# Second batch's transposes one step later, ScalarE counting the experts' tokens, and some sums made by accumulating transfers

## The chip, the cores and the metric

One Trainium2 chip, of which one core is used. The time is the device time of one execution in microseconds (us). The kernel before has a median of 761.44 us over three runs (760.91 to 762.48).

## What is computed

Linear attention with an exponential feature map (4 batches, 8 heads, 576 tokens, head size 64), then a token-mixing sum and a feed-forward block, then a mixture of 8 experts in which every token's expert comes from a running choice. Cut to what matters here:

```python
x = attention(q, k, v, w_phi)                  # [4, 576, 512]
u = x + (x.T @ U @ V).T                        # token mixing, rank 32
x = u + relu(u @ w_ch1) @ w_ch2                # feed-forward, 2048 hidden
logits = x @ w_gate                            # 8 experts
e[s] = argmax(logits[s]) if local_gate[s] < 0.5 or s == 0 else e[s - 1]
out[s] = p[e] * (relu(x[s] @ w1[e]) @ w2[e])
```

## The kernel before

**Precision.** A matrix that goes to TensorE is split in two words: the high one is a copy rounded to the matmul's type, the low one is the value minus the high word. A product is three matmuls (high by high, high by low, low by high), recorded at L1169 to L1171 for the first products of a unit and L1495 to L1497 for the second ones. The high word is a copy on ScalarE (ACT), the low word a subtraction on VectorE (DVE) or GpSimd (POOL). For the experts' second weights (`w_end`, L389) there is already another way: ACT writes minus the high word into the low word's place (L387), and a transfer that POOL issues adds the value to it.

**Items.** The feed-forward block is 4 units of hidden columns times 3 tiles of 768 tokens: items 0 to 11. The experts are 4 batches times 2 units: items 12 to 19. An item is a row of steps. A step is one block product (12 matmuls) of the first layer or a group of 12 matmuls of the second. A seven-product scheme for 2 by 2 blocks replaces eight block products by seven in most items, at the price of sums and differences on DVE. In the last feed-forward unit (items 9, 10 and 11) the second layer uses it too: `seven_steps` and then `z_steps`, 14 steps of which each is a product of 384 columns. Item 12, the first of the experts, is plain: 16 steps with 288 columns.

**The end of a z item.** After the last product DVE adds PSUM and `u2` into the tile `u3` (L1457). What is then still missing in `y`, the block's output, is `u2` on one piece and `u3` on two pieces of 2 by 384 columns. `rest` adds them on DVE, 128x768 each (`from_sbuf`, L1410), and hands copies of `y` to the queue of SyncE (SP) (`sent`, L1415). In items 9 and 10 `rest` is run early in the next item, in item 11 at its end. `ys`, the copy in DRAM, is read only by a loop at the end that runs for batches with more than one expert.

**Routing.** `route(b)` finds batch b's experts in eleven parts: logits on TensorE (L1552), transposes (L1559), small DVE and ACT operations (L1576 to L1595), transposes back (L1606) with copies on ACT (L1610), a scan along the tokens on DVE (L1613), the count of each expert's tokens on DVE (L1617), a product (L1620), transfers (L1624 to L1628), and the choice of the expert (L1633). `PLANS[b]` gives for each part the step at which it is put into the programs of the engines, counted in sixteens from the batch's first item: items 10, 11, 12, 13 for batches 0 to 3. The second batch's part with L1606 stands at 21, that is item 12, step 5; the third batch's logits stand at 2, that is item 12, step 2, and read the tokens 1152 to 1727 of `y`.

**Order of the work.** The kernel is scheduled by hand. All engines' programs are written out in one pass. A planner in Python keeps a clock for each engine (`free`), for each buffer (`touched`) and for the DMA engines (`transfer`), and lets side work (weights, `x` blocks) into an engine's program at a step (`side`, `gate`, `either`) when its planned end is at most a slack behind TensorE's planned clock. `PLAN_COST` tells it what each part of the routing costs DVE, ACT and TensorE. Every engine then works through its program in order and waits at semaphores. `x_end` makes the high and low words of an `x` block; for the first expert batch (`("m", 0)`) there are four blocks of 128x576, made from `y`.

Of the kernel before, what the change touches and what calls it, by code (L numbers as in the profile page):

```python
# [8 lines left out]
F32R = mybir.dt.float32r  # L9
U32 = mybir.dt.uint32  # L10
I32 = mybir.dt.int32
ACTF = mybir.ActivationFunctionType
ALU = mybir.AluOpType
# [30 lines left out]
def model(ctx, tc, kq, vx, wphi, ident, up, vp, wff, wg, wmoe1, wmoe2, rconst, outT):  # L44
# [13 lines left out]
    def f32(ap):  # L58
        return ap.bitcast(F32)
# [14 lines left out]
    def paused(eng, **kw):  # L74

        eng.tensor_tensor(**kw)  # L76
        if eng is nc.gpsimd and pauses[0] and free["POOL"] >= landed[0]:
            nc.gpsimd.drain()
# [107 lines left out]
    def cost(eng, n):  # L186
        return {"DVE": 0.085 + n / 960, "ACT": 0.17 + n / 1330, "POOL": 0.05 + n / 340}[eng]
# [12 lines left out]
    def gate(eng, dur, *keys):  # L200

        if not late:
            yield "step"
        while late and not force[0]:
            at = max([free[eng], port[0] if eng == "DVE" else 0.0] + [touched.get(id(k), 0.0) for k in keys])
            if at + (0.0 if eng == "POOL" else dur) <= free["PE"] + SLACK[eng][at_step[0]]:
                break
            yield "wait"
        emitted[0] += 1
        force[0] = False  # L210
        if late:
            if eng == "DVE":
                free[eng] = max(free[eng], port[0])
            at = book(eng, dur, *keys)
            if eng == "DVE":
                port[0] = at

    def either(eng, n, *keys):

        if not late:  # L220
            yield "step"
            emitted[0] += 1
            return eng
        while True:
            best = None
            for e, name, bias in ((nc.gpsimd, "POOL", 0.0), (nc.vector, "DVE", BIAS)):
                dur = cost(name, n)
                at = max([free[name], port[0]] + [touched.get(id(k), 0.0) for k in keys])
                ok = (name == "DVE" or not lean[0]) and at + (0.0 if name == "POOL" else dur) <= free["PE"] + SLACK[name][at_step[0]]
                if (ok or force[0] and (name == "DVE" or not lean[0])) and (best is None or at + dur + bias < best[0]):  # L230
                    best = (at + dur + bias, e, name, dur)
            if best is not None:
                break
            yield "wait"
        emitted[0] += 1
        force[0] = False
        free[best[2]] = max(free[best[2]], port[0])
        port[0] = book(best[2], best[3], *keys)
        return best[1]

    def transfer(kb, at=None):

        wire[0] = max(free["PE"] if at is None else at, wire[0]) + kb / 400
        return wire[0] + 2.5
# [394 lines left out]
    def spot(key, s):  # L639
# [2 lines left out]
        w = CH if key[0] == "m" else TW  # L642
        return slice(2 * k, 2 * k + 2), slice((2 * key[1] + t) * w, (2 * key[1] + t + 1) * w)

    def x_end(key, s, r, keep, own=None, then=None):

        x = xo.setdefault(key, {})[s] = yield from take(xfree)
        wanted[1] -= then is not None and key[0] == "f"
        n_ = CH if key[0] == "m" else TW
        keys = (x,) if own is None else (x, own)  # L650
        yield from gate("ACT", cost("ACT", 2 * n_), *keys)
        nc.scalar.copy(out=x[:, 0, :, :n_], in_=r)
        for k in (slice(0, 2),) if late else (slice(0, 1), slice(1, 2)):
            use = yield from either(nc.gpsimd, n_ * (k.stop - k.start), *keys)
            paused(use, out=x[:, 1, k, :n_], in0=r[:, k], in1=f32(x[:, 0, k, :n_]), op=ALU.subtract)
        if keep:
            def send():
                nc.sync.dma_start(out=f32(xd[key[1]][XD.index(s)]), in_=f32(x))
                if late:
                    transfer(768)  # L660
            later(x, send)
        xdone.add((key, s))
        if then is not None:
            then()

    def as_x(r):
        return r.rearrange("p (k t) -> p k t", k=2)
# [533 lines left out]
    def seven_steps(i):  # L1201
# [140 lines left out]

        late["rest"] = rest

    def z_item(i):
        return items[i][0].kind == "ffn" and items[i][0].g in ZU

# [29 lines left out]
    def z_steps(i):  # L1377

        u, b = items[i]
        zr, zx = zd["zr"], zd["zx"]  # L1380
        p1, u3 = late["u2"], late["u3"]
        at, done = {}, {}

        def ys(r, t):
            t0 = (2 * b + t) * TW
            return y[:, 2 * r:2 * r + 2, t0:t0 + TW]

        def product(w, x, name, first):
            wt, xt_ = need_w(u, "z" + w), zx[x]
            for j in range(2):  # L1390
                if first:
                    ps, m = bank()
                    done[name, j] = (ps[:, :TW], m)
                    free["PE"] = max(free["PE"], ps_at[m])
                ps, m = done[name, j]
                if not first:
                    free["PE"] = max(free["PE"], ps_at[m])
                at[name, j] = three(ps, wt, xt_, j, first, True, True)
            if last[u] == i:
                wfree.append(u.w.pop("z" + w))  # L1400
            (hfree if any(zx[x] is h for h in hall) else xfree).append(zx.pop(x))

        def to_y(name, r, t):
            for j in range(2):
                ps, m = done[name, j]
                dst = ys(r, t)[:, j]
                ps_at[m] = dve(TW, at[name, j], out=dst, in0=ps, in1=dst, op=ALU.add)

        def from_sbuf(src, r, t, op=ALU.add):
            dve(2 * TW, 0.0, src, out=ys(r, t), in0=ys(r, t), in1=as_x(src), op=op)  # L1410

        def sent(r):
            for d in (2 * r, 2 * r + 1):
                ts_ = slice(2 * b * TW, (2 * b + 2) * TW)
                waiting.append((free["DVE"] + SYNC, lambda d=d: nc.sync.dma_start(out=late["ys"][:, d, ts_], in_=y[:, d, ts_])))  # L1415

        product("A11", "B11", "a", True)
        yield
        for j in range(2):
            ps, m = done["a", j]  # L1420
            ps_at[m] = act(lambda: nc.scalar.copy(out=p1[j], in_=ps), TW, at["a", j])
        touched[id(late["u2w"])] = ps_at[m]
        z_sub("T2", "B22", "T1")
        rows.append(zr.pop("T1"))
        z_high("T2")
        product("S1", "T1", "e", True)
        yield
        to_y("e", 1, 0)
        zd["less"]("T4", "e", "T2")
        z_high("T4")  # L1430
        z_low("T2")
        rows.append(zr.pop("T2"))
        product("A12", "B21", "a", False)
        yield
        zd["less"]("T3", "d", "B22")
        rows.append(zr.pop("B22"))
        z_high("T3")
        z_low("T4")
        rows.append(zr.pop("T4"))
        to_y("a", 0, 1)  # L1440
        product("S4", "B22", "e", False)
        yield
        to_y("e", 0, 0)
        z_low("T3")
        rows.append(zr.pop("T3"))
        product("S2", "T2", "b", True)
        yield
        to_y("b", 0, 0)
        product("A22", "T4", "d", True)
        yield  # L1450
        to_y("d", 1, 1)
        product("S3", "T3", "b", False)
        yield
        assert not zr and not zx
        for j in range(2):
            ps, m = done["b", j]
            ps_at[m] = dve(TW, at["b", j], late["u3w"], out=u3[j], in0=ps, in1=p1[j], op=ALU.add)  # L1457

        def rest(part):
            if part == 0:  # L1460
                from_sbuf(late["u2w"], 0, 0)
                sent(0)
            else:
                for t in range(2):
                    from_sbuf(late["u3w"], 1, t)
                sent(1)

        zd["rest"] = rest
        if not (i + 1 < n and z_item(i + 1)):
            for part in range(2):  # L1470
                z_rest(part)
# [71 lines left out]
    def route(b):  # L1543
# [70 lines left out]
        yield  # L1614

        cnt = small("cnt", [8, 1])
        nc.vector.tensor_reduce(out=cnt, in_=ta, axis=AX, op=ALU.add)  # L1617
        yield

        nc.vector.tensor_tensor(out=tp, in0=tp, in1=ta, op=ALU.mult)  # L1620
# [26 lines left out]
        nc.sync.dma_start(out=scale[b][:, :S], in_=mine[b][bass.ds(ereg[b], 1)].partition_broadcast(128))  # L1647

    routes = []
    PLANS = ((3, 10, 12, 16, 17, 18, 19, 20, 20, 21, 24), (10, 17, 18, 19, 20, 21, 22, 24, 26, 27, 30), (2, 5, 7, 9, 11, 14, 16, 18, 20, 22, 25), (2, 5, 7, 9, 11, 14, 16, 18, 20, 22, 25))  # L1650
    PLAN_COST = ((0.0, 0.8, 1.2), (1.4, 0.0, 0.6), (0.6, 0.0, 0.0), (0.7, 0.0, 0.0), (0.6, 0.0, 0.0), (0.0, 2.3, 0.6), (1.4, 0.0, 0.0), (0.75, 0.0, 0.0), (0.75, 0.0, 0.0), (0.0, 0.0, 0.0), (1.2, 0.0, 0.0))

    def side(i, step, steps):

# [284 lines left out]
```

## Time and profile before

| | |
|---|---|
| median of three runs | 761.44 us |
| profiled execution, its own time | 759.52 us |
| its span, first to last instruction | 757.7 us |
| TensorE busy | 743.6 us (98%) |
| VectorE busy | 629.2 us (83%) |
| ScalarE busy | 373.0 us (49%) |
| GpSimd busy | 99.6 us (13%) |
| granted clock of TensorE over the span | 1.00 of full speed |

The busy time of a matmul is modelled, so a wait of TensorE is best read from the starts of successive matmuls: with 384 columns they lie 0.17 us apart where nothing is waited for, with 288 columns 0.13 us. In a row of the timeline the idle time of the engine ahead of an instruction stands in brackets with what ended it.

### The profile page before, as it was taken

The page shows a single profiled execution, that of the slowest core. Times are in us where ns is not written, and L with a number is a line of the kernel's source. Part 1 is how long each engine was busy: PE and PEld are TensorE (multiplying, and loading weights), DVE is VectorE, ACT ScalarE, POOL GpSimd, SP SyncE. Part 2 cuts the span into 40 slices and gives each one's busy share as a digit, 9 for nine tenths or more (in the row PEclk, how much of TensorE's full clock was granted, in tenths as well). Part 3 has the DMA queues.
Part 4 walks back from the last instruction along what each step waited for, and adds up shares of the span by engine and source line. Part 5 has one row for each costly group of instructions (what it writes and reads, how often), then busy time and mean ns, then how long its engine had stood idle before and what let it go on. Part 6 is the DMA issues. An engine that isn't in the chain of part 4 may idle for free. (4 is left out here: it accounts for less than half of the span.)

```text
span 757.7 us, 18777 instructions
## 1 busy us (share of the span) xinstructions
PE 743.6 (98%) x7644; PEld 721.8 (95%) x7644; DVE 629.2 (83%) x1258; ACT 373.0 (49%) x807; POOL 99.6 (13%) x148
## 2 busy tenths in 40 slices
PE   7999999999999999999999999999999999999997
PEld 6899998999999999999999999999889999999997
DVE  7899999777579999999799476889987797997955
ACT  5677867664242443323323133344557467566560
POOL 0212323122110000100101001010012111011110
PEclk9999999999999999999999999999999999999999
DMA  6444746324479897940569005472287376376861
GB/s 205 157 126 140 267 162 216 98 70 179 154 266 333 295 347 273 351 142 28 195 233 320 3 1 183 149 251 84 72 232 174 75 195 156 87 202 140 203 148 65
DMA packets 57050, 132.15 MB, mean 174 GB/s; under 512 B 5953, under 2 KB 29633, under 8 KB 56961
## 3 DMA queue, kind: packets, MB, share of 16 engines
q1 hardware_dynamic: 42736, 86.68, 33.7%
q0 software_dynamic: 10768, 40.79, 19.2%
q10 hardware_dynamic: 3456, 3.46, 1.4%
q8 instruction: 61, 1.00, 0.6%
q14 instruction: 29, 0.23, 0.1%
HBM read 88.55 MB, written 33.96 MB: 162 GB/s over the span
## 5 line engine op out<-in xcount | busy, mean ns | idle before, releaser
L1169 PE MATMUL psf<-x,w 128*128 128x384 f32 (+1 forms) x576 | 184.5, 320 | 0.5 <-DVE psf L1130 0.5
L1170 PE MATMUL psf<-x,w 128*128 128x384 f32 (+1 forms) x576 | 184.1, 320 | 0.6 <-POOL x L76 0.6
L1171 PE MATMUL psf<-x,w 128*128 128x384 f32 (+1 forms) x576 | 183.9, 319 | 0.0
L1495 PE MATMUL psf<-h,w 128*128 128x384 f32 (+1 forms) x544 | 171.8, 316 | 0.0
L1496 PE MATMUL psf<-h,w 128*128 128x384 f32 (+1 forms) x544 | 171.5, 315 | 0.0
L1497 PE MATMUL psf<-h,w 128*128 128x384 f32 (+1 forms) x544 | 171.5, 315 | 0.0
L1169 PEld LDWEIGHTS psf<-x,w 128*128 128x128 f32 x576 | 108.3, 188 | 2.2 <-issue 0.9
L1170 PEld LDWEIGHTS psf<-x,w 128*128 128x128 f32 x576 | 108.2, 188 | 1.0 <-POOL x L76 0.9
L1171 PEld LDWEIGHTS psf<-x,w 128*128 128x128 f32 x576 | 108.2, 188 | 0.0
L1495 PEld LDWEIGHTS psf<-h,w 128*128 128x128 f32 x544 | 102.1, 188 | 0.1
L1496 PEld LDWEIGHTS psf<-h,w 128*128 128x128 f32 x544 | 102.1, 188 | 0.0
L1497 PEld LDWEIGHTS psf<-h,w 128*128 128x128 f32 x544 | 102.1, 188 | 0.0
L1147 ACT ACTIVATE h<-psf 128x384 fp32r<-128x384 f32 (+1 forms) x136 | 58.5, 454 | 86.8 <-DVE psf L1130 55.0
L1130 DVE TENSOR_TENSOR y<-psf,y 128x384 f32<-128x384 f32 (+1 forms) x134 | 69.4, 527 | 24.8 <-PE psf L1497 21.2
L1132 DVE SCALAR_TENSOR_TENSOR h<-psf,h 128x384 fp32r<-128x384 f32 (+1 forms) x142 | 66.0, 505 | 20.5 <-ACT h L1147 19.8
L384 ACT CAST w<-row 128x512 fp32r<-128x512 f32 x62 | 36.9, 618 | 51.6 <-DVE row L373 26.2
L757 POOL DMA_DIRECT2D x<-xd x41 | 21.9, 534 | 269.5 <-PE psf L1171 232.6
L1130 DVE TENSOR_TENSOR u<-psf,p 128x384 f32<-128x384 f32 (+1 forms) x64 | 32.3, 514 | 24.5 <-PE psf L1171 23.7
L858 DVE TENSOR_REDUCE mx<-pj 128x6 f32<-128x768 f32 (+2 forms) x49 | 45.8, 934 | 6.1 <-PE pj L855 5.9
L859 DVE TENSOR_TENSOR pg<-pj,mx 128x768 f32<-128x768 f32 (+2 forms) x49 | 46.1, 941 | 2.5
L888 PE MATMUL kv<-vt,ek 128*64 128x65 f32 (+1 forms) x1152 | 47.1, 230 | 0.7 <-DMA vt<-in_vx 0.7
L373 DVE TENSOR_TENSOR w<-row,w 128x512 fp32r<-128x512 f32 x56 | 37.5, 686 | 9.2 <-ACT w L384 9.2
(141 smaller groups left out, 1240.9 us busy)
## 6 DMA issues: line engine op xcount, KB each, us to landing
x<-xd POOLq DMA_DIRECT2D x41, 768.0 KB, 6.5
raw<-in_wff SPq DMA_DIRECT2D x32, 512.0 KB, 3.8
xd<-x SPq DMA_DIRECT2D x21, 768.0 KB, 5.1
raw<-in_wmoe SPq DMA_DIRECT2D x52, 256.0 KB, 3.7
kq<-in_kq SPq DMA_DIRECT2D x14, 576.0 KB, 4.7
w<-raw POOLq DMA_DIRECT2D x26, 256.0 KB, 4.3
vt<-in_vx SPq DMA_DIRECT2D x16, 325.0 KB, 2.9
ud<-y SPq DMA_DIRECT2D x4, 1152.0 KB, 6.8
```

The costliest lines, as they stand in the source:

```text
L858: nc.vector.tensor_reduce(out=mx[:, :, sl], in_=ps[:, :, sl], axis=AX, op=ALU.max, apply_absolute_value=True)
L859: nc.vector.tensor_tensor(out=p[:, :, sl], in0=ps[:, :, sl], in1=mx[:, :, sl].unsqueeze(3).to_broadcast([128, 2, m, 128]), op=ALU.subtract)
L888: nc.tensor.matmul(out[c], lhsT=e[:, half, i, c], rhs=rhs, start=(tl == 0 and half == 0), stop=(tl == 8 and half == 1), skip_group_check=True)
L1130: nc.vector.tensor_tensor(**kw)
L1132: nc.vector.scalar_tensor_tensor(op1=op1, **kw)
L1147: hat[t, f] = act(lambda: nc.scalar.activation(out=hhi, in_=src, func=ACTF.Relu), n_, ready)
L1169: nc.tensor.matmul(ps, lhsT=w[:, 0, c], rhs=x[:, 0, k, :n_], start=(first and k == 0), stop=False, skip_group_check=True)
L1170: nc.tensor.matmul(ps, lhsT=w[:, 0, c], rhs=x[:, 1, k, :n_], start=False, stop=False, skip_group_check=True)
L1171: nc.tensor.matmul(ps, lhsT=w[:, 1, c], rhs=x[:, 0, k, :n_], start=False, stop=(stop and k == 1), skip_group_check=True)
L1495: nc.tensor.matmul(ps, lhsT=wh, rhs=hhi, start=(k == 0), stop=False)
L1496: nc.tensor.matmul(ps, lhsT=wl, rhs=hhi, start=False, stop=False)
L1497: nc.tensor.matmul(ps, lhsT=wh, rhs=hlo, start=False, stop=(k == 3))
```

## The change

Five edits. (1) The low words of the four `x` blocks of the first expert batch are made by an ACT multiplication and an accumulating transfer that POOL issues, in place of a subtraction on DVE or POOL. (2) In items 10 and 11 the two additions of `u3` into `y` become two accumulating transfers, issued by POOL at the end of the item; item 9 (`ZFIRST`) keeps them on DVE; the copies to `ys` of these pieces are due at the planned landing. (3) The count of an expert's tokens is taken by ACT, as the accumulated sum of a copy. (4) The second batch's plan is moved by one step from its sixth part on. (5) The planner's cost of the count moves from DVE to ACT.

```diff
+    def x_low(x, r, keys, n_):
+        for k in (slice(0, 2),) if late else (slice(0, 1), slice(1, 2)):
+            use = yield from either(nc.gpsimd, n_ * (k.stop - k.start), *keys)
+            paused(use, out=x[:, 1, k, :n_], in0=r[:, k], in1=f32(x[:, 0, k, :n_]), op=ALU.subtract)
...
         nc.scalar.copy(out=x[:, 0, :, :n_], in_=r)
-        for k in (slice(0, 2),) if late else (slice(0, 1), slice(1, 2)):
-            use = yield from either(nc.gpsimd, n_ * (k.stop - k.start), *keys)
-            paused(use, out=x[:, 1, k, :n_], in0=r[:, k], in1=f32(x[:, 0, k, :n_]), op=ALU.subtract)
+        if late and key[0] == "m" and key[1]==0:
+            yield from gate("ACT", cost("ACT", 2 * n_), *keys)
+            nc.scalar.mul(out=x[:, 1, :, :n_], in_=f32(x[:, 0, :, :n_]), mul=-1.0)
+            yield from gate("POOL", 0.6, *keys)
+            nc.gpsimd.dma_start(out=x[:, 1, :, :n_], in_=r.bitcast(F32R), accum_op=ALU.add)
+            at = max(transfer(576, free["POOL"]), free["POOL"] + ADD_LAT)
+            for k in keys:
+                touched[id(k)] = at
+        else:
+            yield from x_low(x, r, keys, n_)
...
+    ZFIRST = NP * ZU[0]
...
-                waiting.append((free["DVE"] + SYNC, lambda d=d: nc.sync.dma_start(out=late["ys"][:, d, ts_], in_=y[:, d, ts_])))
+                at_ = free["DVE"] + SYNC if not r or i == ZFIRST else touched[id(late["u3w"])] + SYNC
+                waiting.append((at_, lambda d=d: nc.sync.dma_start(out=late["ys"][:, d, ts_], in_=y[:, d, ts_])))
...
-                for t in range(2):
-                    from_sbuf(late["u3w"], 1, t)
+                if i == ZFIRST:
+                    for t in range(2):
+                        from_sbuf(late["u3w"], 1, t)
                 sent(1)
+        if i != ZFIRST:
+            for t in range(2):
+                nc.gpsimd.dma_start(out=ys(1, t), in_=as_x(late["u3w"]), accum_op=ALU.add)
+                free["POOL"] = max(free["POOL"], free["DVE"] + SYNC) + 0.6
+                touched[id(late["u3w"])] = max(transfer(384, free["POOL"]), free["POOL"] + ADD_LAT)
...
-        nc.vector.tensor_reduce(out=cnt, in_=ta, axis=AX, op=ALU.add)
+        nc.scalar.activation(out=tk, in_=ta, func=ACTF.Copy, accum_out=cnt)
...
     PLANS (second batch)
-    (10, 17, 18, 19, 20, 21, 22, 24, 26, 27, 30)
+    (10,17,18,19,20,22,24,25,27,28,31)
     PLAN_COST (eighth part)
-    (0.75, 0.0, 0.0)
+    (0.0, 0.75, 0.0)
```

## Rows read from the trace of the kernel before

**Rows 1.** The page, part 1: busy us, share of the span, instructions.
```profile
PE 743.6 (98%) x7644; PEld 721.8 (95%) x7644; DVE 629.2 (83%) x1258; ACT 373.0 (49%) x807; POOL 99.6 (13%) x148
```

**Rows 2.** Waits of TensorE from 480 us on: us in total, times, longest.
```profile
PE psf L1606 <- DVE tr L1595: 1.8, 1, 1.8
PE psf L1170 <- DVE h L1130: 0.7, 2, 0.4
PE psf L1169 <- DVE psf L1130: 0.5, 1, 0.5
```

**Rows 3.** Timeline of TensorE: start us, us, engine, line, instruction, count [idle before].
```profile
532.13 0.34 PE L1171 MATMUL psf<-x,w 128*128 128x384 f32 x1
532.96 0.44 PE L1169 MATMUL psf<-x,w 128*128 128x384 f32 x1 [0.49 <-DVE psf L1130]
...
535.80 0.44 PE L1170 MATMUL psf<-h,w 128*128 128x384 f32 x1 [0.32 <-DVE h L1130]
...
552.26 0.29 PE L1169 MATMUL psf<-x,w 128*128 128x288 f32 x1
...
557.65 1.18 PE L1552 MATMUL psf<-y,wg_sb 128*32 128x288 f32 x16
...
563.49 0.29 PE L1171 MATMUL psf<-x,w 128*128 128x288 f32 x1
565.55 0.71 PE L1606 MATMUL psf<-id_sb,tr 128*72 128x128 f32 x5 [1.77 <-DVE tr L1595]
```

**Rows 4.** Timeline of VectorE, item 11, around the first late product.
```profile
527.94 1.35 DVE L1613 TENSOR_TENSOR_SCAN row<-row,row 8x576 f32<-8x576 f32 x1 [0.74 <-ACT row L1610]
529.21 0.98 DVE L1130 TENSOR_TENSOR u<-psf,p 128x384 f32<-128x384 f32 x2
...
531.02 0.74 DVE L1617 TENSOR_REDUCE r_cnt<-row 8x1 f32<-8x576 f32 x1
...
532.35 1.01 DVE L1130 TENSOR_TENSOR psf<-psf,u 128x384 f32<-128x384 f32 x2
...
534.79 0.96 DVE L1130 TENSOR_TENSOR h<-row,h 128x768 fp32r<-128x768 f32 x1 [0.50 <-ACT h L1364]
```

**Rows 5.** Timeline of ScalarE, item 11.
```profile
532.93 0.95 ACT L1239 ACTIVATE row<-psf 128x384 f32<-128x384 f32 x2 [2.82 <-DVE psf L1130]
```

**Rows 6.** Timeline of VectorE, end of item 11 and item 12.
```profile
549.39 0.74 DVE L76 TENSOR_TENSOR x<-y,x 128x576 fp32r<-128x576 f32 x1
...
553.39 1.00 DVE L1130 TENSOR_TENSOR u<-psf,u 128x384 f32<-128x384 f32 x2
554.33 2.67 DVE L1130 TENSOR_TENSOR y<-y,u 128x768 f32<-128x768 f32 x3
...
565.20 0.20 DVE L1595 TENSOR_TENSOR tr<-r_ex,r_sm 128x40 f32<-128x40 f32 x1
```

**Rows 7.** Accumulating weight transfers (L389), issued from 545 to 585 us.
```profile
DMA to landing us min/median/max: 3.3/4.2/5.0
```

**Rows 8.** Issues of DMAs, whole span: KB each, median us to landing.
```profile
ud<-y SPq DMA_DIRECT2D x4, 1152.0 KB, 6.8
```

**Rows 9.** The 384 KB copies `ys<-y` (L1415), first 520 to 530 us.
```profile
DMA to landing us min/median/max: 2.9/2.9/2.9
```

**Rows 10.** The same copies, 552 to 560 us.
```profile
DMA to landing us min/median/max: 3.6/4.3/5.0
```

**Rows 11.** Stretch 552.1 to 557.65: busy us per engine, clock, DMA share, GB/s.
```profile
552.10:557.65 5.55, 5.55 (x44) 5.39 (x43) 5.55 (x10) 1.39 (x3) 0.00 (x0) 1.00 1.03 318
```

**Rows 12.** The 768 KB loads `x<-xd` that POOL issues (L757), whole span.
```profile
DMA to landing us min/median/max: 4.5/6.5/10.2
```

**Rows 13.** VectorE at the end of item 10.
```profile
518.80 1.24 DVE L1130 TENSOR_TENSOR u<-psf,u 128x384 f32<-128x384 f32 x2
```

**Rows 14.** GpSimd, its first transfer after 501 us.
```profile
533.06 0.52 POOL L1624 DMA_DIRECT2D mine<-row  x1 [32.29 <-issue]
```

**Rows 15.** ACT multiplication by -1 of 128x512 (L387), 540 to 600 us: ns min/median/max.
```profile
L387 ACT ACTIVATE w<-w x9: 631/632/652, 549.7 to 599.8; 128x512 fp32r<-128x512 f32 x9
```

More of the change, by code (lines that the diff above doesn't have):

```diff
@@ L1649, in model @@
     routes = []
-    PLANS = ((3, 10, 12, 16, 17, 18, 19, 20, 20, 21, 24), (10, 17, 18, 19, 20, 21, 22, 24, 26, 27, 30), (2, 5, 7, 9, 11, 14, 16, 18, 20, 22, 25), (2, 5, 7, 9, 11, 14, 16, 18, 20, 22, 25))
-    PLAN_COST = ((0.0, 0.8, 1.2), (1.4, 0.0, 0.6), (0.6, 0.0, 0.0), (0.7, 0.0, 0.0), (0.6, 0.0, 0.0), (0.0, 2.3, 0.6), (1.4, 0.0, 0.0), (0.75, 0.0, 0.0), (0.75, 0.0, 0.0), (0.0, 0.0, 0.0), (1.2, 0.0, 0.0))
+    PLANS = ((3, 10, 12, 16, 17, 18, 19, 20, 20, 21, 24), (10,17,18,19,20,22,24,25,27,28,31), (2, 5, 7, 9, 11, 14, 16, 18, 20, 22, 25), (2, 5, 7, 9, 11, 14, 16, 18, 20, 22, 25))
+    PLAN_COST = ((0.0, 0.8, 1.2), (1.4, 0.0, 0.6), (0.6, 0.0, 0.0), (0.7, 0.0, 0.0), (0.6, 0.0, 0.0), (0.0, 2.3, 0.6), (1.4, 0.0, 0.0), (0.0, 0.75, 0.0), (0.75, 0.0, 0.0), (0.0, 0.0, 0.0), (1.2, 0.0, 0.0))
     def side(i, step, steps):
```

## The prediction

> **What bounds the kernel now.** Read the page's busy shares first. TensorE is busy for 743.6 of 757.7 us, and the other engines clearly less [rows 1]. The change touches no matmul, so it can give back only time in which TensorE waits. The list of TensorE's waits comes next. All edits act from item 10's end on, and from 480 us to the end there are four waits: once 1.8 us for the sums that the second batch's transposes read (L1606), once 0.5 us for a sum in PSUM, and two waits of 0.7 us together for low words of the hidden block [rows 2]. TensorE's timeline gives the exact loss. A matmul of 384 columns follows the last one after 0.17 us, so the one at 532.96 is 0.66 us late; one of 288 columns follows after 0.13 us, so the transposes at 565.55 are 1.93 us late [rows 3]. The two low-word waits, each a little longer between starts than its idle time, are some 0.5 us each. All four together, 3.6 us, are the most that can be won. The question is which go, and which wait comes in their place.
>
> **The sum wait at 532.96.** Read VectorE's timeline. The scan starts at 527.94 because ScalarE's copies of the first batch's transposes end there, and from then on VectorE has no idle time up to the sum at 532.35 that TensorE waits for [rows 4]. So what the change takes off VectorE before 527.94 (three low words of `x`, the two additions of `u3`) only makes that idle time longer. The one removed instruction inside the stretch is the count at 531.02, 0.74 us long; instructions overlap a little, so the sum moves up by some 0.67 us. This just covers the lateness: gain 0.65 us. ScalarE gets the count in a gap in which it waits 2.82 us for that same sum [rows 5], and it must only pass after the scan, at 529.3. Were it as long as 1 us, the gap would still hide it; without the gap every relu behind it would be late by its length.
>
> **The two low-word waits.** The second product of this chain waits for a low word that starts at 534.79, after VectorE itself idled for ScalarE [rows 3, 4]: sum, relu, copy, difference, one behind the other. When the sum comes 0.67 us earlier, TensorE also comes 0.65 us earlier, and the chain between them is as long as before. I take no gain, with 1.0 us as the other end.
>
> **The transposes at 565.55.** They are put one step later, behind one more product. Between 552.26 and 557.65 lie three products and five transposes of some 0.5 us [rows 3], so a product is 1.6 us. The sums end at 565.40 [rows 6]. TensorE's old arrival was 563.62. In the new order it is 563.62, less 0.65 from above, plus 1.6 for the product, plus 0.5 for the third batch's transposes, which now come first: 565.1, and later by whatever TensorE loses in between. VectorE reaches these sums earlier too, since two of the three additions at 554.33 (2.67 us) are gone [rows 6]. So the whole 1.93 us goes. What comes late next: the scan, count and choice of batch 1 move by one step, and its weights are needed only two items on.
>
> **The new wait.** The two additions in item 11 become transfers, and the first of them writes tokens 1536 to 1919 of `y`. The third batch's logits read tokens up to 1727 in their second half, so they must wait for its landing. In the old order VectorE ended all three additions at 557.00, 0.65 us before the logits start [rows 3, 6]. In the new one:
> - TensorE needs the piece at 557.65 plus half of the logits' issue (0.55), less 0.65: 557.55.
> - The `u3` sums ended at 554.39. Ahead of them VectorE loses the count and one low word of `x` (549.39, 0.74), 0.7 us each: 553.0. TensorE's product ends at 551.6 in the new order, so 552.1 is the earliest; if weights' low words fill the room again, 553.7 [rows 3, 6].
> - No row shows an accumulating transfer of 384 KB. The 256 KB ones of this stretch take 3.3 to 5.0 us to land, median 4.2 [rows 7]. Size: 1152 KB take 6.8 us and 384 KB take 2.9 in a quiet stretch, 0.65 us per 128 KB [rows 8, 9]. Crowding: from 552.1 to 557.65 the DMA engines are full (share 1.03) [rows 11], and the same 384 KB copies then take 4.3 in place of 2.9 [rows 9, 10]; the 4.2 holds part of that, so I add half, 0.7. Together 5.5 us. The ends are 3.3, the fastest accumulation, and 10.2, the slowest transfer that POOL issued [rows 7, 12].
> - Landing 558.5, wait 1.0 us. With the ends: none, or 5.6 us.
>
> The Trainium skill, "DMA: Bandwidth & Descriptors", section "Anatomy of one DMA — SWDGE (gpsimd) path", fits such a transfer as 2.0 us plus bytes over 436 GB/s, an estimate of 2.9 us for this one. By it the piece would land at 556.0 and the logits would not wait at all; for 256 KB it gives 2.6 us where the rows have 4.2, so I don't use it in the sum.
>
> **Edits that I cost at nothing.** The same transfers in item 10: the `u3` sums end at 520.04 [rows 13], POOL is free, having nothing to issue until 533 [rows 14], and two landings of 5.5 us, the second 1 us behind, end by 526.6. VectorE writes `u3` again at 529.21 [rows 4], so 2.6 us are spare; past that each us is VectorE's and then TensorE's. The four low words by transfer: ScalarE does four more multiplications of some 0.7 us (0.63 for 512 columns [rows 15]), three of them before 532, where it waits anyway [rows 5]. The transfers queue on POOL behind those of `y` and ahead of the weights'; three land near 530, long before item 12. The fourth, made at 549.39 before [rows 6], is wanted in the second half of item 12's third product, at 551.6 + 3.2 + 0.5 + 0.8 = 556.1; issued as late as 549.4 it lands at 554.9. If it were later, TensorE would wait for the difference. The copies to `ys` on SP now wait for the landing, some 1.5 us past the old end of the additions, and the loads of weights behind them on SP with them; those weights belong to item 13. The changed planner costs reorder side work in items 11 to 14. I cost that at nothing, with 0.5 us either way.
>
> **Sum.** -0.65 - 1.93 + 1.0 = -1.6 us, on the execution's own 759.52: 757.9. The median of the runs lies 1.92 us above that execution. I carry the difference over: 761.44 - 1.6, or 759.9 with rounding up.
>
> **Rivals.**
> - *No new wait.* The piece lands within 4.5 us, as most of the 256 KB ones do [rows 7]. For it: a quiet 384 KB copy takes 2.9 [rows 9]. Against it: full DMA engines at that moment [rows 11]. Gain 2.6 us: 758.9. The rule quoted above comes out here.
> - *All four waits go.* It needs the chain sum, relu, copy, difference to shrink, and nothing of it is removed. Gain up to 3.6: 757.9.
> - *A late landing eats the gain.* With 6.5 to 8.7 us to landing the logits wait 2.0 to 4.1 us: 760.8 to 763.0.
> - *Slower: the accumulation of `y` is far slower than that of the weights.* One mechanism and one place, the third batch's logits: every us of landing past 4.5 is a us of TensorE. The gain is gone at 7.1 us and the kernel is slower by over 0.2% from 8.7 us. At 10.2 the wait is 5.6 and the time 764.5. For it: loads that POOL issued took up to 10.2 [rows 12], and this transfer has pieces of 1.5 KB where the weights' has 2 KB. Against it: those loads have twice the bytes.
> - *The moved step doesn't do what it says.* If VectorE's sums stayed at 565.40 and TensorE arrived at 565.1, 0.3 us of the wait would be left. This is inside the forecast's range.
>
> **Chances.** 0.2% (1.5 us) is about what a measurement here can tell from no change: faster means below 759.92, slower above 762.96. Forecast, landing 4.5 to 6.5 us, 758.9 to 760.8: 0.45, of which 0.24 lie below 759.92. No new wait 0.18. All four go 0.06. Late landing 0.17. Slower 0.14. So faster 0.24 + 0.18 + 0.06 = 0.48, same 0.21 + 0.17 = 0.38, slower 0.14. The range for 8 in 10 leaves out the case of all four and nearly all of slower: 758.7 to 762.4.
>
> **What would show it.** After: no wait of the second batch's transposes for DVE; the matmul near 532.3 on time; the two low-word waits still there; a wait of L1552 for a transfer into `y` near 557.6, of about 1 us. A landing of L1410's successor below 4.5 or above 6.5 us, a wait of VectorE for it in item 11, or a wait of TensorE in the first products of item 12 for an `x` block would make the prediction wrong.

## The result, and the profile after

The changed kernel is slower: 766.69 us median (764.55 to 767.19), against 761.62 for the kernel before on the same chip. The ratio is 1.0062, with a 95% interval of 1.005 to 1.0074. The forecast was 759.9 and its range ended at 762.4, so the prediction was wrong, and on the other side of no change. The profiled execution took 764.55 us, with a span of 762.8; that is 5.03 us over the profiled execution of before (759.52). It is the fastest of the four and has a mean granted clock of 0.997; the other three have 0.994 to 0.996. By these rounded means the lower clock costs them 0.8 to 2.3 us more (an estimate: difference of the means times the span), a good part of the 1.9 to 2.6 us that they are longer.

First the busy shares of the page, part 1, of the changed kernel, which answer to [rows 1]:

```profile
span 762.8 us, 18785 instructions
PE 746.2 (98%) x7644; PEld 723.8 (95%) x7644; DVE 620.9 (81%) x1246; ACT 378.2 (50%) x819; POOL 109.1 (14%) x156
```

TensorE has the same 7644 matmuls and is yet busy 2.6 us longer. Matmuls got slower somewhere, which no edit asks for. Next, TensorE's waits from 480 us on (us in total, times, longest), which answer to [rows 2]:

```profile
PE psf L1574 <- DMA y<-u: 2.8, 1, 2.8
PE psf L1182 <- DVE u L1143: 0.7, 1, 0.7
PE psf L1183 <- DVE h L1143: 0.7, 2, 0.4
PE psf L1518 <- DMA w<-raw: 0.6, 1, 0.6
PE psf L1182 <- DVE psf L1143: 0.3, 1, 0.3
```

L1574 are the third batch's logits (L1552 before), L1182 and L1183 the products (L1169 and L1170), L1518 the second layer, L1628 the transposes (L1606). The transposes' wait is gone, as forecast. In its place the logits wait for the accumulating transfer into `y`, and there are two waits that I did not see coming: for VectorE's sums `u` at 619.7, and for a low word of a weight at 722.6. TensorE's timeline (start us, us, line, shape, count, and the idle time before) gives the size of the first one and what follows it; it answers to the end of [rows 3]:

```profile
557.83 1.16 PE L1574 MATMUL psf<-y,wg_sb 128*32 128x288 f32 x12
561.84 0.68 PE L1574 MATMUL psf<-y,wg_sb 128*32 128x288 f32 x4 [2.84 <-DMA y<-u]
562.45 0.40 PE L1182 MATMUL psf<-x,w 128*128 128x288 f32 x1
562.69 0.29 PE L1183 MATMUL psf<-x,w 128*128 128x288 f32 x1
562.82 0.29 PE L1184 MATMUL psf<-x,w 128*128 128x288 f32 x1
...
563.49 0.44 PE L1183 MATMUL psf<-x,w 128*128 128x288 f32 x1
563.73 0.44 PE L1184 MATMUL psf<-x,w 128*128 128x288 f32 x1
563.97 0.44 PE L1182 MATMUL psf<-x,w 128*128 128x288 f32 x1
```

The last four of the logits' sixteen matmuls, which read the awaited piece, start 3.24 us later than one logits matmul follows another. From 563.49 a product's matmul follows the last one after 0.24 us and not 0.13. The table by stretch (busy time of each engine, then granted clock, DMA share and GB/s) says why:

```profile
554.00:560.00 6.00, 4.99 (x43) 4.05 (x41) 3.29 (x10) 3.78 (x9) 3.03 (x3) 1.00 1.07 295
560.00:561.80 1.80, 0.00 (x0) 0.00 (x0) 1.66 (x7) 0.08 (x1) 0.23 (x1) 1.00 1.06 262
561.80:563.40 1.60, 1.56 (x11) 1.10 (x12) 0.74 (x1) 0.84 (x2) 0.00 (x0) 1.00 1.17 207
563.40:566.90 3.50, 3.50 (x17) 3.50 (x17) 1.37 (x7) 1.64 (x4) 0.94 (x2) 0.51 0.98 192
566.90:568.00 1.10, 1.10 (x10) 1.10 (x10) 0.54 (x2) 0.54 (x2) 0.75 (x1) 1.00 1.03 394
```

Behind the wait the granted clock is at its lower level, 1.2 GHz, for some 3.4 us. Fourteen matmuls cost 3.36 us there and not 1.85: another 1.5 us. The logits lose a little more than their wait, because their matmuls then start in pairs and not in fours. From their first matmul to the next product they take 4.62 us (557.83 to 562.45), and before 1.10 (557.65 in [rows 3] to this row of before), 0.28 us more than the 3.24:

```profile
558.75 0.40 PE L1169 MATMUL psf<-x,w 128*128 128x288 f32 x1
```

GpSimd's timeline shows the transfers (it answers to [rows 14]):

```profile
520.68 2.46 POOL L1487 DMA_DIRECT2D y<-u  x2 [19.56 <-DVE r_fr L1609]
522.17 5.81 POOL L663 DMA_DIRECT2D x<-y  x4
...
550.34 0.89 POOL L389 DMA_DIRECT2D w<-row  x1 [16.01 <-ACT w L387]
554.19 2.40 POOL L1487 DMA_DIRECT2D y<-u  x2 [2.97 <-DVE u L1143]
```

VectorE's timeline in item 11, at the place where the forecast saw 2.6 us to spare ([rows 4]), shows a wait for the second one of item 10:

```profile
528.27 1.34 DVE L1635 TENSOR_TENSOR_SCAN row<-row,row 8x576 f32<-8x576 f32 x1 [3.67 <-ACT row L1632]
530.04 1.02 DVE L1143 TENSOR_TENSOR u<-psf,p 128x384 f32<-128x384 f32 x2 [0.42 <-DMA y<-u]
```

The first transfer of item 10 (issued at 520.68) and the first of item 11 (554.19) among the DMA issues, KB and us from issue to landing:

```profile
y<-u POOLq DMA_DIRECT2D x1, 384.0 KB, 4.6
...
y<-u POOLq DMA_DIRECT2D x1, 384.0 KB, 7.6
```

The sum of the profiled executions, in us: transposes -1.93; the sum at 533 -0.18; the logits' wait +3.24; the lower clock +1.5; 619.7 +0.87; 722.6 +0.79. That is +4.3 of the +5.0; a further 0.33 is a shift that TensorE already has before the matmul at 533, 0.28 is the rest of the logits' loss, and 0.1 I can't place.

### The profile page after: what moved, and what is told of

Read it like the earlier page. It is cut to its first block, busy times and chain, and to the rows that moved or that the text cites. A ratio compares the mean times of both kernels' runs of the same rounds, so it can differ in the third digit from the quotient of the medians.

```text
span 762.8 us, 18785 instructions
## 1 busy us (share of the span) xinstructions
PE 746.2 (98%) x7644; PEld 723.8 (95%) x7644; DVE 620.9 (81%) x1246; ACT 378.2 (50%) x819; POOL 109.1 (14%) x156
## 5 line engine op out<-in xcount | busy, mean ns | idle before, releaser
L1182 PE MATMUL psf<-x,w 128*128 128x384 f32 (+1 forms) x576 | 185.7, 322 | 1.0 <-DVE u L1143 0.7
L1183 PE MATMUL psf<-x,w 128*128 128x384 f32 (+1 forms) x576 | 184.8, 321 | 0.6 <-POOL x L76 0.6
L1518 PE MATMUL psf<-h,w 128*128 128x384 f32 (+1 forms) x544 | 171.9, 316 | 0.6 <-DMA w<-raw 0.6
L1182 PEld LDWEIGHTS psf<-x,w 128*128 128x128 f32 x576 | 109.1, 189 | 3.0 <-DVE u L1143 0.9
L1183 PEld LDWEIGHTS psf<-x,w 128*128 128x128 f32 x576 | 109.0, 189 | 1.0 <-POOL x L76 0.9
L1518 PEld LDWEIGHTS psf<-h,w 128*128 128x128 f32 x544 | 102.2, 188 | 0.9 <-DMA w<-raw 0.9
```

The costliest lines, as they stand in the source:

```text
L1182: nc.tensor.matmul(ps, lhsT=w[:, 0, c], rhs=x[:, 0, k, :n_], start=(first and k == 0), stop=False, skip_group_check=True)
L1183: nc.tensor.matmul(ps, lhsT=w[:, 0, c], rhs=x[:, 1, k, :n_], start=False, stop=False, skip_group_check=True)
L1518: nc.tensor.matmul(ps, lhsT=wl, rhs=hhi, start=False, stop=False)
```

## Experiments

Theory: the slowdown is item 11's transfer of `y`, which lands under TensorE's reader, with the lower clock that follows. Rivals: the moved plan, the other transfers, or the copies and loads behind the late landing. Each median is of 6 to 12 executions, but for the first row (four) and the last (one). The ratio is to the kernel before, timed beside it on the same chip; every trace is of one execution. "Landing" is of item 11's first transfer of `y`, "lost" is how much later TensorE's matmul starts at the logits.

| run | kernel | median us | ratio, 95% interval | landing | lost |
|---|---|---|---|---|---|
| after | the change | 766.69 | 1.0062 (1.005 to 1.0074) | 7.60 | 3.24 |
| e1 | item 11's additions on VectorE | 760.3 | 0.9973 (0.9958 to 0.9987) | none | 0 |
| e2 | before + moved plan | 763.31 | 1.0011 (0.9999 to 1.0024) | none | 0 |
| e3 | before + `y` by transfer | 769.88 | 1.0097 (1.0073 to 1.0121) | 8.52 | 4.86 |
| e4 | before + low words of `x` by transfer | 761.48 | 0.999 (0.9979 to 1.0001) | none | 0 |
| e5 | item 10's copies held | 765.84 | 1.0042 (1.0028 to 1.0057) | 8.18 | 3.86 |
| e6 | logits three steps later | 764.75 | 1.0031 (1.0019 to 1.0044) | 8.25 | 0 |
| e9 | e2 + stores on SP | 760.06 | 0.9973 (0.9958 to 0.9987) | none | 0 |
| e10 | item 10: one of two | 765.93 | 1.0039 (1.0026 to 1.0052) | 8.16 | 3.96 |
| e11 | item 11's copies held | 762.84 | 1.0017 (1.0002 to 1.0032) | 7.07 | 2.71 |
| e14 | item 11: the first alone | 763.24 | 1.0017 (1.0004 to 1.0031) | 7.00 | 2.67 |
| e12 | item 11: the second alone | 760.52 | 0.9987 (0.9976 to 0.9999) | 7.10 (the second) | 0 |
| e13 | e9 + count on ScalarE | 758.8 | 0.9969 (0.9958 to 0.998) | none | 0 |
| e20 | after + stores on SP | 765.45 | 1.0057 (1.0045 to 1.007) | 8.82 | 4.50 |
| e15 | e1 + stores on SP | 759.58 | 0.9974 (0.9962 to 0.9986) | none | 0 |
| e16 | e11 + loads of weights held | 769.75 (one run) | | 4.99 | 0.66 |

**e1: the last item's additions back on VectorE.**

```diff
...
-                if i == ZFIRST:
+                if i != ZFIRST + 1:
                     for t in range(2):
                         from_sbuf(late["u3w"], 1, t)
...
-        if i != ZFIRST:
+        if i == ZFIRST + 1:
             for t in range(2):
                 nc.gpsimd.dma_start(out=ys(1, t), in_=as_x(late["u3w"]), accum_op=ALU.add)
```

The cut part gives item 11's copies their old due time again.

> The changed kernel with one thing undone: item 11's two additions of u3 into y are on VectorE again (item 10's stay transfers). Theory A (the loss is the third batch's logits waiting 3.2 us for item 11's first transfer, and the half clock of 3.4 us that follows, 1.5 us): the wait of the logits for a transfer is gone, the clock stays at full speed through items 11 to 13, and the time falls by about 4.7 us from the changed kernel's, to some 762 us. Rival B (the planner's new order of side work and the transfers of x cost it): the time stays within 1 us of the changed kernel's 766.7.

760.3 us, 6.4 below the changed kernel (4.7 was expected) and below the kernel before. The clock is full throughout, and neither the logits nor the transposes wait; the wait at 619.7 is gone as well:

```profile
PE psf L1518 <- DMA w<-raw: 1.1, 1, 1.1
PE psf L1183 <- DVE h L1143: 0.7, 2, 0.3
PE psf L1182 <- DVE psf L1143: 0.4, 1, 0.4
```

So item 11's two transfers, with what follows from them, turn a faster kernel into a slower one.

**e2: the moved plan alone.**

```diff
-    PLANS = (..., (10, 17, 18, 19, 20, 21, 22, 24, 26, 27, 30), ...)
+    PLANS = (..., (10,17,18,19,20,22,24,25,27,28,31), ...)
```

> The kernel before with the second batch's plan alone moved by one step. Theory A: the 1.9 us wait of its transposes goes and nothing comes in its place: 759.7 us, 1.9 below before. Rival B (moving the plan reorders the side work of items 12 to 14 so that other waits come): 761 or more, with new waits of TensorE between 610 and 730 us.

763.31 us, and not 759.7, as rival B had it. The transposes' wait is gone and another has come, 54 us further on. Its waits from 480 us, and below them the stretch behind the new one, where the granted clock (third number from the end) is at the lower level:

```profile
PE psf L1169 <- DVE u L1130: 2.0, 1, 2.0
PE psf L1170 <- DVE h L1130: 0.7, 2, 0.3
PE psf L1169 <- DVE psf L1130: 0.5, 1, 0.5
PE psf L1496 <- DMA w<-raw: 0.2, 1, 0.2
```

```profile
620.20:623.70 3.50, 3.50 (x18) 3.50 (x17) 3.43 (x8) 0.82 (x2) 0.56 (x1) 0.51 0.98 207
```

ScalarE's timeline ahead of that wait, and under it VectorE's:

```profile
612.42 0.36 ACTq L1540 DMA_DIRECT2D outT<-y  x1
612.82 0.74 ACT L1610 COPY row<-psf 8x256 f32<-8x256 f32 x2 [2.06 <-DVE y L1529]
...
614.97 1.03 ACTq L1540 DMA_DIRECT2D outT<-y  x2
616.04 0.62 ACT L384 CAST w<-row 128x512 fp32r<-128x512 f32 x1 [0.81 <-issue]
```

```profile
616.70 0.69 DVE L373 TENSOR_TENSOR w<-row,w 128x512 fp32r<-128x512 f32 x1 [1.74 <-ACT w L384]
617.30 0.45 DVE L1130 TENSOR_TENSOR y<-psf,y 128x288 f32<-128x288 f32 x1
617.67 1.33 DVE L1613 TENSOR_TENSOR_SCAN row<-row,row 8x576 f32<-8x576 f32 x1
618.94 0.78 DVE L1130 TENSOR_TENSOR u<-psf,p 128x288 f32<-128x288 f32 x2
```

ScalarE stands behind a store of finished rows that waits for VectorE's scaling (2.06 us); its cast of a weight comes late; VectorE stands 1.74 us before that cast, and the sums `u` behind it are TensorE's. e9 tests this reading.

**e3: the transfers of `y` alone**, without the edits to plan, count and `x`.

> The kernel before with the additions of u3 into y by transfer in items 10 and 11 alone. Theory A: the third batch's logits wait some 3 us, the clock halves for 3 to 4 us (1.5 us), and the old wait of the transposes (1.9) vanishes behind it: 2.5 to 3.5 us slower than before, 764 to 765. Rival C (it was the four transfers of x in the same queue that made the landing late): the landing takes 5.5 us or less, the logits wait 1 us or less, and the time is at most that of before.

769.88 us, the slowest of all that were timed more than once, and 5 us above theory A's range, which had neither so long a wait (4.86 us lost) nor so long a stretch at the lower clock. The low words of `x` by transfer do not make the landing late: without them it is later still (8.52 us). Half clock lasts 6.8 us here, and a wait of 2.29 us comes near 626.

**e4: the low words of `x` alone.**

> The kernel before with the low words of the four x blocks by transfer alone. Theory A: nothing on TensorE's path changes: within 0.8 us of before, all four waits of TensorE as before. Rival C (the transfers crowd the DMA engines or POOL's queue and delay something else): slower by 1 us or more, with a wait of TensorE that ends at a transfer.

761.48 us, the same as before within the interval. Taking these low words off VectorE buys nothing that can be measured, as forecast.

**e5 and e10: aimed wrongly.** Their condition `i == ZFIRST + 1` names item 10, the second of the three items concerned, and not item 11 of which the expectations speak.

```diff
-                at_ = free["DVE"] + SYNC if not r or ...
+                at_ = free["DVE"] + SYNC + (10.0 if i == ZFIRST + 1 else 0.0) if not r or ...
```

> The changed kernel, only that two 384 KB copies of item 11 (ys, upper half), which SP issues at 554.8 and 555.2 beside the first accumulating transfer of y (issued 554.19, landed 561.79, 7.60 us), are held back until the transfers have landed. Theory A (crowding: the copies share the DMA engines with the transfer): it lands in 4.5 to 5.2 us as the one of item 10 did (4.57 us), the logits wait at most 0.8 us, the clock stays full, time 761.5 to 763. Rival B (the two accumulating transfers and what they read and write set their own pace, whatever goes beside them): landing 7 us or more, the logits wait over 2.5 us, time within 1 us of the changed kernel's 766.7.

```diff
+            if i == ZFIRST + 1:
+                from_sbuf(late["u3w"], 1, 0)
-            for t in range(2):
+            for t in (1,) if i == ZFIRST + 1 else (0, 1):
                 nc.gpsimd.dma_start(out=ys(1, t), in_=as_x(late["u3w"]), accum_op=ALU.add)
```

> The changed kernel, only that in item 11 the first of the two additions of u3 (tokens 1536 to 1919, which the logits read) is VectorE's again and the second stays a transfer. Theory A (only the first piece meets a reader in time): no wait at the logits, full clock, time as with both on VectorE (760.3) or up to 1 us less: 759.3 to 760.5. Rival B (one late transfer is enough to hold up SP's copies and the weights behind them, or VectorE's next use of u3): a new wait of 1 us or more behind 560, time 762 or more.

Neither expectation was tested. They say something else: with item 10's copies held or one of its transfers gone, item 11's transfer still takes 8.2 us and the kernel stays slow (1.0042 and 1.0039). So neither these copies nor this transfer of item 10 sets item 11's landing. They show one thing more: the wait for the sum at 533 is gone in both. With item 10's copies held the second transfer of item 10 lands 6.13 us after its issue and not 8.49.

**e6: the reader later.**

```diff
-    PLANS = (..., (2, 5, 7, 9, 11, 14, 16, 18, 20, 22, 25), ...)
+    PLANS = (..., (5, 6, 8, 9, 11, 14, 16, 18, 20, 22, 25), ...)
```

> The changed kernel, only that the third batch's logits come three steps later in item 12 (two entries of its plan follow one step later each). It takes the reader of y out of the landing's way and leaves the transfers as they are. Theory A (the time is lost at the logits' wait, 3.24 us, and in the 1.5 us of half clock behind it): neither is there, 762.0 (761 to 763), with waits of 0.9 us near 619 and 0.8 us near 722 left as they are or moved by the planner. Rival B (the late transfers cost by what stands behind them: copies, loads of weights on SP, low words on POOL): 765 or more, with other waits in items 12 to 14.

764.75 us, between the two. The logits' wait and the lower clock behind it are gone in the trace, and the third batch's moved plan brought waits of its own: 1.47 us for the transposes at 609.6, 1.72 us for the sums at 618.2, and two of 0.5 us. It doesn't tell the theories apart.

**e9: stores of finished rows on SP**, on top of e2.

```diff
-            eng = nc.scalar if keep else nc.sync
+            eng = nc.sync
```

> The kernel before with the second batch's plan moved (763.3 us alone, with a new wait of 2.2 us for VectorE's sums at 619.4 and half clock from 620.2), only that the stores of the finished output rows are issued by SP and not by ScalarE. Theory A (ScalarE stands behind a store that waits for VectorE's scaling, so its casts of weights come late, and VectorE, whose next instruction needs such a cast, makes its sums late): the wait at 619 is gone or under 0.5 us, full clock, time 759.6 (759 to 761). Rival B (the planner gives VectorE more work ahead of those sums, whatever ScalarE does): the wait stays near 2 us, time 763 to 764.

760.06 us, as the theory had it. The wait near 619 shrinks from 2.0 to 0.2 us and the clock is full. ScalarE, which in e2 had a store at 612.4 ahead of the copies, now runs straight into the cast:

```profile
608.78 2.42 ACT L1610 COPY row<-psf 8x256 f32<-8x256 f32 x6
611.10 0.61 ACT L384 CAST w<-row 128x512 fp32r<-128x512 f32 x1
```

**e11: item 11's copies behind the landing** (as e5, with `ZFIRST + 2`).

> The changed kernel, only that item 11's own two copies to ys (upper half, 384 KB each, issued by SP 0.6 and 1.0 us behind the first accumulating transfer of y) come behind the next loads of weights, past the landing. Theory A (crowding by these copies): the first transfer lands in 4.6 to 5.2 us, as item 10's does (4.57 to 4.67 us, nothing issued beside it but the second one), the logits wait at most 0.8 us, full clock, time 761.5 to 763. Rival B (the pair of transfers sets its own pace there): landing 7 us or more, the logits' wait over 2.5 us, 765.5 to 767.

Landing 7.07 us, wait 2.71 us at full clock in the profiled execution, 762.84 us. The landing is 0.5 us shorter than in the changed kernel; the time is in the first theory's range, but not by its mechanism. Without the copies the DMA engines are as full as with them, since five loads of weights, which SP issued from 551.06 to 556.00, go on. The transfer among the DMA issues, and then the table by stretch (554 to 560 us, share 1.09):

```profile
y<-u POOLq DMA_DIRECT2D x1, 384.0 KB, 7.1
```

```profile
554.00:560.00 6.00, 5.80 (x49) 4.86 (x47) 3.92 (x11) 2.97 (x7) 2.40 (x2) 1.00 1.09 248
```

**e14 and e12: one piece by transfer**, the first or the second (as e10's diff, with `ZFIRST + 2`, and for e14 with the pieces exchanged).

> The changed kernel, only that in item 11 the second addition of u3 (tokens 1920 to 2303) is VectorE's again, so one accumulating transfer goes alone, beside the two copies. Theory A (the two copies crowd it): landing stays at 7 us or more, the logits wait 2.5 us or more, 765 to 767. Rival B (its twin, issued 0.74 us behind, shares its pace): landing 4.6 to 5.5 us, wait of 1 us at most, 761.5 to 763.

Landing 7.00 us without a twin, wait 2.67 us at full clock, 763.24 us. The copies come only at 557.7 in this run, 2.5 us behind the transfer. So the twin isn't the cause either.

> The changed kernel, only that in item 11 the first addition of u3 (tokens 1536 to 1919, which the logits read) is VectorE's again; the second stays a transfer. Theory A (only the piece with an early reader costs): no wait at the logits, full clock, 759.3 to 760.6 (both on VectorE: 760.3). Rival B (one late transfer is enough to hold up SP's copies and the loads behind them, or VectorE's addition falls behind its queue): a new wait of 1 us or more behind 560, 762 or more.

760.52 us, no wait at the logits, though the piece lands in 7.10 us. A slow landing without an early reader costs nothing that the intervals of e12 and e1 can tell (0.9987 and 0.9973).

**e16: the loads of weights held too** (five loads of the third batch's weights follow the held copies on SP).

> The changed kernel with item 11's own copies to ys behind the landing (with that alone the first transfer took 7.07 us), and with the five loads of the third batch's weights that SP issues from 551.7 us on held back behind the second transfer as well. It is a look at one landing; the weights come some 10 us late, so the time may be anything from 761 to 770. Theory A (those loads share the DMA engines with the transfer, busy share 1.05 to 1.16 from 554 to 562): the first transfer lands in 4.5 to 5.3 us as in item 10 and the logits wait 0.9 us at most. Rival B (what stretches it is the low word of weights that POOL issued 4 us ahead of it, or something of the place): 6.5 us or more, wait over 2 us.

The landing is 4.99 us and the logits lose 0.66 us: with the loads held the transfer is nearly as fast as in item 10. The transfer among the DMA issues, and then the table by stretch, where the DMA share is 0.63:

```profile
y<-u POOLq DMA_DIRECT2D x1, 384.0 KB, 5.0
```

```profile
554.00:560.00 6.00, 5.74 (x50) 4.66 (x49) 4.67 (x15) 2.43 (x6) 2.40 (x2) 1.00 0.63 103
```

That speaks for the loads, on one execution. One rival goes with it: a low word of weights that GpSimd issued some 4 us ahead on its own queue landed 0.53 us before the transfer's issue here, and 0.90 us behind it in e11. In e14 it landed later still, 2.03 us behind, and the transfer took 7.00 us as in e11, which speaks against it; no run holds that low word alone. The two copies alone don't do it: in item 10 of the changed kernel, too, two of 384 KB go 1.4 us behind the first transfer, and it lands in 4.57 us; there nothing was in flight when it was issued.

The Trainium skill, "DMA: Bandwidth & Descriptors", section "SWDGE vs HWDGE vs iDMA", says that transfers issued by GpSimd and those issued by SP or ScalarE sit in different queues of each DMA engine, which serves them by turns; the pair e11 and e16, 7.07 and 4.99 us, agrees with it. Holding the loads is no way out, since the weights then come late:

```profile
PE psf L1518 <- DMA w<-raw: 4.2, 1, 4.2
PE psf L1517 <- ACT w L384: 1.4, 1, 1.4
PE psf L1574 <- DMA y<-u: 0.3, 1, 0.3
```

**e13, e20, e15: stores on SP** in three surroundings.

> The kernel before with the second batch's plan moved, the count on ScalarE, and the stores of finished rows on SP; no added transfers. With the first and third of these alone: 760.06 us, ratio 0.9973, and one wait of 0.65 us for a sum in PSUM near 534. Theory A (the count's 0.74 us on VectorE is what makes that sum late): the wait shrinks by 0.2 to 0.65 us, 759.5 us, ratio 0.9965 (0.995 to 0.998). Rival B (with the count moved the planner puts other work in another order and a wait comes back in items 12 to 14): 761 or more.

758.8 us, the fastest: the moved plan, the count on ScalarE, stores on SP, and no added transfer. The wait for the sum in PSUM is gone, and one line is left from 480 us on:

```profile
PE psf L1183 <- DVE h L1143: 0.7, 2, 0.3
```

> The changed kernel, only that the stores of finished rows are issued by SP. Theory A (the wait of 0.87 us near 619 comes from ScalarE standing behind such stores): that wait is gone or under 0.3 us, the logits' wait and the half clock stay, 765.8 us (0.9 less; 765 to 766.5). Rival B (SP's loads come late behind the stores): waits for weights in its place, 767 or more.

765.45 us: the wait near 619 is gone, and the logits' wait stays (4.50 us lost in the profiled execution).

> All parts of the change but item 11's two additions, which stay on VectorE (760.3 us, ratio 0.9973), and the stores on SP. Theory A (the transfers of item 10 and of the low words of x bring nothing that the moved plan, the count and the stores on SP don't bring, and add a late low word of weights): 759.5 to 760.5, not below the 758.8 us (ratio 0.9969) of the kernel without any added transfer. Rival B (VectorE's freed time takes another wait away): under 758.5.

759.58 us: as expected. With item 10's transfers and those of `x` kept, nothing is gained over e13, and a wait of 1.4 us for a low word of the hidden block at 622.6 takes the place of e1's at 718.

## Why the prediction was wrong, step by step

- **The sum at 532.96: -0.65 forecast, -0.18 measured.** The failing step is "2.6 us are spare" for item 10's transfers. The prediction put the second landing 1 us behind the first, near 526.6; in fact the second came 8.49 us after its issue, at 529.92, and VectorE, ready to write `u3` at 529.62, waited 0.42 us for it. That ate what the count gave. It is the copies to `ys` beside it that made it so late: with them held (e5) it lands in 6.13 us and the wait is gone. In e13, which has the count on ScalarE and no such transfer, the wait is gone: the count's part of the step was right.
- **The two low-word waits stay.** Right: 0.49 and 0.54 us lost.
- **The transposes: -1.93.** Right, in e1 and e2. In the changed kernel the wait is gone too, but there TensorE comes late anyway.
- **The new wait: +1.0 forecast, 3.24 measured.** This is the step that decided. Place, reader and mechanism were named rightly; the landing was mis-sized, 5.5 us in the sum and 7.60 measured, and in it the term for crowding. Two smaller errors nearly cancel. The transfer was issued at 554.19 and not at 553.0, because low words of weights filled VectorE's room again, an end that the prediction names:

```profile
552.29 0.67 DVE L373 TENSOR_TENSOR w<-raw,w 128x512 fp32r<-128x512 f32 x1
552.89 1.00 DVE L1143 TENSOR_TENSOR u<-psf,u 128x384 f32<-128x384 f32 x2
```

And TensorE came to the awaited matmuls at 558.60 (561.84 less 3.24) and not at 557.55, because the 0.65 was not won, the shift of 0.33 came on top, and the reader is the last quarter of the logits and not their second half. So 2.10 for the landing, 1.19 for the issue and -1.05 for the reader make the 2.24 by which the wait is longer. That 4.2 plus 0.65, 4.85, lies near item 10's 4.57 and e16's 4.99 is luck: the 4.2 came from a busy stretch and was to hold part of the crowding. Against 0.7 us for crowding the runs show 2.1 that go with the loads of weights (e11's 7.07 less e16's 4.99) and 0.5 to 1.8 more in the kernels that keep the copies early (7.60 to 8.82). I had taken the crowding from copies that SP issued, 2.9 to 4.3 us [rows 9, 10], and halved it, because the 256 KB rows [rows 7] hold some of it already; the accumulating transfer loses 2.4 to 4.3 us against 4.57, where those copies lost 1.4. Of my two ends the slow one, `x<-xd` from POOL with its 6.5 us in the median [rows 12], was the nearer. The Trainium skill, "DMA: Bandwidth & Descriptors", section "Anatomy of one DMA — SWDGE (gpsimd) path", gives 2.9 us as an estimate for this size; no run here is below 4.51 us, with nothing in flight at the issue, and under load it is less than half of what is measured.
- **What a wait costs: not in the sum at all.** I counted each us of the wait as a us of TensorE. The lower clock behind it added 1.5. No wait in the trace of before was followed by it, so its rows could not show the price; they could show that from 480 us on none was as long (1.93 us lost at most).
- **Edits at nothing.** The low words of `x`: right (e4), though all four were issued by 525.66 and landed from 531.66 to 538.84, where the prediction had three near 530. The planner's reordering, 0 with 0.5 either way: wrong. It brought 0.87 us in the changed kernel and 2.2 us with the plan alone, through a store on ScalarE's queue in item 14 (e2, e9, e20). Where the 0.79 us at 722.6 come from was not tested. I had followed the moved step to the next item and not to the stores two items on.
- **The rivals.** "A late landing eats the gain" (6.5 to 8.7 us, waits of 2.0 to 4.1) is what happened. Its times ended at 763.0 because they knew neither the clock (1.5) nor the waits in items 14 and later (1.66), nor that the 0.65 would be lost (0.47). Of the 6.6 us between forecast (757.9) and the profiled execution (764.55), the longer wait is 2.24 and these three are 3.6; of the 0.8 left the shift is 0.33, the rest of the logits' loss 0.28, and 0.2 stays open.

Not shown: why the same transfer takes 7.6 in one kernel and 8.2 to 8.8 in others whose order on the queues is the same or nearly so. And whether a wait of TensorE is followed by the lower clock can't be told from its length alone in these runs, nor from one execution (last section).

## What to carry to other kernels

When an addition is given to a transfer, price the landing from the slowest transfer of that queue in the same busy stretch, look at what is in flight when it is issued, and ask who reads the piece first: the same landing of 7.1 us cost 2.7 us of wait where the logits read it and none where they did not. Moving a step by one product can change the queues several items on, so look there for stores or casts behind which another engine stands. Here the gain lay in the parts without transfers (plan, count, stores on another queue: 758.8 us, ratio 0.9969).

## What the runs showed of the hardware

- An accumulating transfer of 384 KB within SBUF landed in 4.51 to 4.67 us when nothing was in flight at its issue, and in 7.0 to 8.8 us where loads of weights were. A second one issued 0.74 us behind the first landed 2.2 (e5, item 10's copies held) to 4.7 us (after) behind it in item 10, yet in item 11 the first was no faster alone (7.00 against 7.07 us).
- In the profiled executions TensorE's granted clock fell to 1.2 GHz late in the wait or at most 2 us behind it where the wait lost 3.24 us (after), 3.86 (e5), 3.96 (e10), 4.44 (e16), 4.50 (e20) or 4.86 us (e3), and stayed there for some 3.4 to 6.8 us. It stayed full behind waits of 2.71 (e11), 2.67 (e14), 2.29 (e3) and 1.93 us (before), but in e2 it fell behind one of 2.21 us. It differs between executions of one kernel: 3.4 us at half clock in a span of 764 take 0.0022 off the mean and leave 0.998 at most, and six of e2's twelve executions and one of e5's have 0.999 or 1.000, while two of e11's have 0.996. So one trace shows that the fall can come, not how often it does.
